# Three moves in a fused attention and gated-MLP kernel: a reordered start, product sums spaced differently, and a DRAM reload placed behind weight slabs

## The chip, the cores and the metric

The kernel runs on one core of a Trainium2 chip. The metric is the device time of one execution in microseconds, the median of several runs. Runs of one kernel mostly agree within about 0.1%. Block 0 to block 3 are quarters of 512 tokens of the 2048-token sequence; "slab" is a 1 MB piece of weights in a ring of five buffers.

## The reference, cut to what matters

```python
x = A_x                                              # 1 x 2048 x 1024, bf16
x = x + _A_ref(_layernorm(x), A_wqkv, A_wo)          # attention over 8 keys, 2 apart, 32 heads of 32
x = x + _B_ref(_layernorm(x), W_gate, W_up, W_down)  # relu(x W_gate) * (x W_up), then W_down; 3584 wide
x = x + _A_ref(_layernorm(x), A_wqkv, A_wo)
x = x + _B_ref(_layernorm(x), W_gate, W_up, W_down)
```

## The kernel before: the parts that matter

The kernel is a list of events with planned times. They are sorted and emitted, and each engine's instructions stand in its queue in that order. VectorE's work is chained by `dv`, SyncE's transfers by `sp_dma`. While TensorE does block 0's gate and up projections, VectorE does block 1's attention in between. The scores of block 1 (`s`, product sums of q and k) go through DRAM to be regrouped by head: `store_s`, then `load_s`.

```python
def load_s(n):                         # the reload: 4 transfers, 256 KB each, packets of 256 bytes
    def f():
        sd = s_d[n % 2]
        s4 = work.tile([P, DG, W, P], BF16, tag="t", name=f"s4_{n}")
        for tq in range(TPB):
            src = bass.AP(tensor=sd.tensor, offset=sd.offset + tq * P,
                          ap=[[DG * W * BLK, H], [BLK, DG * W], [1, P]])
            sp_dma(s4[32 * tq:32 * tq + 32, :, :, :].rearrange("p d w t -> p (d w) t"), src)
        att[n]["s4"] = s4
    return f

def head_sum(n):                       # u: what waits for the reload, on VectorE
    s4 = att[n].pop("s4")
    u = work.tile([P, DG // 2, W, P], F32, tag="ac", name=f"u_{n}", bufs=1)
    dv(nc.vector.tensor_tensor, u[:], s4[:, 0:2], s4[:, 2:4], op=ALU.add)
    ...

def gu_steps(n, ln):                   # gate group j and up group j, 8 matmuls of 512 columns each
    ...
            for nm in ("g", "u"):
                acc = psum.tile([P, BLK], F32, tag="acc", name=f"acc_{nm}")   # 6 buffers in all
                ...                                                           # relu on ScalarE
    def gate(j):
        def f():                       # hT(j): frees the up buffer; on VectorE, behind all that is emitted before
            dv(nc.vector.tensor_tensor, hold["hT"][:, j, :], ups.pop(j)[:], rs.pop(j)[:], op=ALU.mult)
        return f
    ...
```

The start, `ln_first`, normalises the first four tiles of 128 tokens, turns them on TensorE and copies them out, while `v_first` already multiplies by the V weights. Its code is in the diff below.

## Time and profile before

| | before |
|---|---|
| median, lowest, highest of all 6 runs | 1617.99, 1617.71, 1619.53 us |
| profiled span | 1616.4 us |
| TensorE busy | 1611.3 us |
| first V matmul; first matmul of the Q projection | 8.09; 24.04 us |
| reload issued; u starts | 233.90; 243.90 us |
| slab w_u(4) issued, lands; its first weight load; its first matmul by the chain | 239.88, 246.9; 247.06; 247.43 us |

The lines of the profile are in the prediction. How to read the table: TensorE never waits after the start, so other engines cost nothing as long as their results are in time. What counts in such a kernel is the slack of each hand-over: by how much a transfer or a VectorE result is early.

### The profile page before, as it was taken

The page shows a single profiled execution, that of the slowest core. Times are in us where ns is not written, and L with a number is a line of the kernel's source. Part 1 is how long each engine was busy: PE and PEld are TensorE (multiplying, and loading weights), DVE is VectorE, ACT ScalarE, POOL GpSimd, SP SyncE. Part 2 cuts the span into 40 slices and gives each one's busy share as a digit, 9 for nine tenths or more (in the row PEclk, how much of TensorE's full clock was granted, in tenths as well). Part 3 has the DMA queues.
Part 4 walks back from the last instruction along what each step waited for, and adds up shares of the span by engine and source line. Part 5 has one row for each costly group of instructions (what it writes and reads, how often), then busy time and mean ns, then how long its engine had stood idle before and what let it go on. Part 6 is the DMA issues. An engine that isn't in the chain of part 4 may idle for free.

```text
span 1616.4 us, 18930 instructions
## 1 busy us (share of the span) xinstructions
PE 1611.3 (100%) x7633; PEld 786.6 (49%) x7633; DVE 1137.1 (70%) x960; ACT 475.8 (29%) x968; POOL 180.4 (11%) x168
## 2 busy tenths in 40 slices
PE   9999999999999999999999999999999999999999
PEld 6646544444444445444454444544445444444444
DVE  5999989996989698929489293893939939311211
ACT  5853312132116313603136031361313311131110
POOL 2400100010003002300053000530005100000000
PEclk9999999999999999999999999999999999999999
DMA  9868868697669766794847947479574794755452
GB/s 306 180 190 238 224 159 262 183 216 204 208 192 217 200 184 212 192 246 146 227 160 201 240 153 230 152 205 252 165 226 155 203 245 157 209 161 177 157 167 68
DMA packets 407448, 317.92 MB, mean 197 GB/s; under 512 B 166464, under 2 KB 387008, under 8 KB 406848
## 3 DMA queue, kind: packets, MB, share of 16 engines
q1 hardware_dynamic: 406784, 316.13, 69.9%
q8 instruction: 59, 0.97, 0.3%
q10 hardware_dynamic: 576, 0.59, 0.1%
q14 instruction: 29, 0.24, 0.0%
HBM read 266.29 MB, written 34.66 MB: 186 GB/s over the span
## 4 chain that ended last, share of the span: by engine, by line
PE 99%; DMA 0%; ACT 0%; DVE 0%; issue 0%; ACTq 0%; DVEq 0%
PE acc_u L132 24%; PE acc_g L132 24%; PE dacc L132 18%; PE acc_v L132 7%; PE acc_wo L132 7%; PE acc_k L132 7%; PE acc_q L132 7%; PE dacc_pair L132 6%; DMA x<-in_A_x_dram 0%; ACT xn_first L328 0%; PE tp_pair L385 0%; PE L L132 0%; DVE x L837 0%; DVE xnT_first L106 0%; ACTq L175 0%
## 5 line engine op out<-in xcount | busy, mean ns | idle before, releaser
L132 PE MATMUL acc_g<-xnT_b,w_g 128*128 128x512 bf16 x1792 | 423.3, 379 | 0.0
L132 PE MATMUL acc_u<-xnT_b,w_u 128*128 128x512 bf16 x1792 | 423.3, 379 | 0.0
L790 ACT ACTIVATE r<-acc_g 128x512 bf16<-128x512 f32 x224 | 133.5, 596 | 726.7 <-PE acc_g L132 701.6
L106 DVE TENSOR_TENSOR hT<-acc_u,r 128x512 bf16<-128x512 f32 x224 | 150.5, 685 | 240.7 <-PE acc_u L132 238.2
L132 PE MATMUL dacc<-w_d,hT 128*128 128x512 bf16 (+1 forms) x1400 | 301.9, 375 | 0.0
L132 PEld LDWEIGHTS <-hT 128*128 128x128 bf16 x1820 | 178.1, 98 | 208.9
L132 PEld LDWEIGHTS <-w_u 128*128 128x128 bf16 x1792 | 175.3, 98 | 211.5
L132 PEld LDWEIGHTS <-w_g 128*128 128x128 bf16 x1792 | 175.4, 98 | 211.4
L106 DVE TENSOR_TENSOR pv<-a,vhm 128x4096 bf16<-128x4096 bf16 x64 | 143.4, 2281 | 0.0
L837 DVE TENSOR_TENSOR x<-dacc,x 128x512 bf16<-128x512 f32 (+1 forms) x38 | 24.5, 672 | 154.2 <-PE dacc L132 154.2
L608 DVE TENSOR_TENSOR t<-q,k 128x2048 f32<-128x2048 bf16 x56 | 128.0, 2292 | 6.7 <-ACT k L543 4.6
L106 DVE TENSOR_TENSOR t<-q,k 128x2048 f32<-128x2048 bf16 x56 | 127.4, 2285 | 3.7 <-ACT k L543 2.6
L106 DVE TENSOR_TENSOR pv<-pv 128x1024 bf16<-128x1024 bf16 (+1 forms) x128 | 113.6, 947 | 0.0
L549 POOL COPY kh<-k 128x14 bf16<-128x14 bf16 x40 | 56.0, 1406 | 504.3 <-ACT k L543 504.3
L132 PE MATMUL acc_wo<-w_o,oT 128*128 128x512 bf16 x512 | 111.8, 379 | 0.0
L621 DVE TENSOR_TENSOR ac<-ac,t 128x2048 f32<-128x2048 f32 x48 | 109.6, 2284 | 0.3
L106 DVE TENSOR_TENSOR ac<-ac,t 128x2048 f32<-128x2048 f32 x48 | 109.5, 2282 | 0.0
L264 POOL TENSOR_TENSOR st_b<-st_b,neg_half 128x1 f32<-128x1 f32 x29 | 43.9, 1523 | 525.8 <-ACT st_b L263 525.7
L132 PE MATMUL dacc_pair<-w_d,hT 128*128 128x512 bf16 x420 | 95.9, 379 | 0.0
L132 PEld LDWEIGHTS <-oT 128*128 128x128 bf16 x512 | 50.0, 98 | 60.4
L259 ACT ACTIVATE xn_b<-x 128x1024 bf16<-128x1024 bf16 x29 | 30.3, 1045 | 129.1 <-DVE x L106 67.0
L446 ACT CAST vT<-acc_v 128x512 bf16<-128x512 f32 x56 | 32.8, 588 | 57.6 <-PE acc_v L132 56.6
(134 smaller groups left out, 1230.0 us busy)
## 6 DMA issues: line engine op xcount, KB each, us to landing
w_g<-in_B_W_gate_dram SPq DMA_DIRECT2D x56, 1024.0 KB, 7.4
w_u<-in_B_W_up_dram SPq DMA_DIRECT2D x56, 1024.0 KB, 5.5
w_d<-in_B_W_down_dram SPq DMA_DIRECT2D x48, 1024.0 KB, 5.7
w_o<-in_A_wo_dram SPq DMA_DIRECT2D x16, 1024.0 KB, 7.0
vhm<-v_d SPq DMA_DIRECT2D x32, 284.0 KB, 6.8
v_d<-vT SPq DMA_DIRECT2D x8, 1024.0 KB, 9.8
oT<-o_d SPq DMA_DIRECT2D x32, 256.0 KB, 4.5
w_d<-in_B_W_down_dram SPq DMA_DIRECT2D x16, 512.0 KB, 3.9
```

What stands on the lines that cost most here:

```text
L106: tail_dve[0] = f(*args, **kwargs).ins
L132: tail_pe[0] = nc.tensor.matmul(*args, **kwargs).ins
L259: nc.scalar.activation(xn, xt[:], ACT.Square, accum_out=sq)
L264: nc.gpsimd.tensor_tensor(rstd, vpe, neg_half[:, 0:1], op=ALU.pow)
L446: tail_act[0] = nc.scalar.copy(st["vT"][:, c, :], acc[:]).ins
L549: nc.gpsimd.tensor_copy(khalo[n][:, c, :], k[:, BLK:BLK + HALO])
L608: nc.vector.tensor_tensor(t[:], i0, i1, op=ALU.mult)
L621: nc.vector.tensor_tensor(o, ac[:], t[:], op=ALU.add)
L790: tail_act[0] = nc.scalar.activation(rs[j][:], acc[:], ACT.Relu).ins
L837: run = dv if n < NB - 2 else (lambda f, *args, **kwargs: f(*args, **kwargs))
```

## The change

The intent: let TensorE start a little earlier (ScalarE copies tile 0 out before it does statistics), and make the up slab w_u(4), which comes at most half a microsecond before it is needed, safe by putting it ahead of the reload. The product sums of block 1 are spaced differently too. The core of the diff:

```diff
-            elif t == 2:
-                nc.scalar.dma_start(x_tiles[t][:], x_dram[t * P:(t + 1) * P, :])
...
-    load_x(0, range(TPB - 1))
+    load_x(0, [0, 1])
...
-                sp_dma(tv[:, rows, :], src[:, rows, :])
+                start = nc.scalar.dma_start if (key[1], i) == (0, 1) else sp_dma
+                start(tv[:, rows, :], src[:, rows, :])
...
     load_slab(("v0", 0), qkv_half(2, 0))
-    load_x(0, [TPB - 1])
+    load_x(0, [2, 3])
...
-        act_square(2)
-        act_mean(2)
         bn(1, 0)
         ...
         copy(0, "a", 0, KC // 4, KC // 2)
+        act_square(2)
+        act_mean(2)
...
-        def second(h):
-            turn(1, (h,))
-            if h == 0:
-                copy(1, "v", 0)
-                return
+        def second():
+            turn(1)
+            copy(1, "v", 0)
             copy(1, "v", 1)
+            bn(3, 0)
+            act_power(2)
+            bn(3, 1)
+            aggr(3)
             apply(2)
-            act_square(3)
-            act_mean(3)
-            act_power(3)
             apply(3)
...
-                if kc == KC // 2 - 1:
-                    ln["second"](0)
                 for c in range(KC):
                     prod(kc, c, 0, 1)
-            ln["second"](1)
+            ln["second"]()
...
-    spread(sums1[6:10], t_fill + 1.4, 4.6)
+    spread(sums1[6:10], t_fill + 3.3, 4.0)
...
-            ev.append((at + 40.5, load_s(1)))
+            ev.append((at + 24 * GRP + 0.5, load_s(1)))
```

I call its three parts the start, the sums (the `spread` line) and the reload (the last line). In the reload part SyncE's order becomes store, two small gets, w_u(4), w_g(5), reload; before it was store, get, reload, get, w_u(4), w_g(5).

More of the change, by code (lines that the diff above doesn't have):

```diff
@@ L373, in ln_first, with turn @@
         tps = {}
-        def turn(t, halves=(0, 1)):
-            if t in tps:
-                pass
-            elif t == 0:
+        def turn(t):
+            if t == 0:
                 tps[t] = [psum.tile([P, KC // 2, P], BF16, tag="acc", name=f"tp{h}")[:] for h in range(2)]
@@ L382, in turn @@
                 tps[t] = [both[:, h, 0:KC // 2, :] for h in range(2)]
-            for c in (h * (KC // 2) + i for h in halves for i in range(KC // 2)):
+            for c in range(KC):
                 with pe_group():
@@ L408, in ln_first @@
         copy(0, "v", 1)
-        act_power(2)
         apply(1, 0)
         apply(1, 1)
-        def second(h):
-            turn(1, (h,))
-            if h == 0:
-                copy(1, "v", 0)
-                return
+        def second():
+            turn(1)
+            copy(1, "v", 0)
             copy(1, "v", 1)
+            bn(3, 0)
+            act_power(2)
+            bn(3, 1)
+            aggr(3)
             apply(2)
-            act_square(3)
-            act_mean(3)
-            act_power(3)
             apply(3)
```

## The prediction

> **What bounds the kernel now.** I read the page first. Its part 1 says that TensorE is busy 1611.3 of 1616.4 us, and its part 4, the chain that ended last, is 99% PE.
>
> ```profile
> PE 1611.3 (100%) x7633; PEld 786.6 (49%) x7633; DVE 1137.1 (70%) x960; ACT 475.8 (29%) x968; POOL 180.4 (11%) x168
> PE 99%; DMA 0%; ACT 0%; DVE 0%; issue 0%; ACTq 0%; DVEq 0%
> ```
>
> A busy PE may still hide gaps, so I took the chain of waits in order of time. From 24.04 us on it is matmuls in steps of 1.73 us for 8 of 512 columns (216 ns each); the 56 groups of block 0's gate and up take 287.15 - 190.45 = 96.70 us, or 56 x 1.727: no gap. The waits of PE in the whole trace are two, both at the start (1.5 and 0.4 us). So time can be won only before 24 us, at most some tenths, and lost anywhere that a buffer or slab becomes late. The start, from the chain (start us, us, what):
>
> ```profile
> 1.25 4.17 DMA x<-in_A_x_dram
> ...
> 5.45 1.16 ACT xn_first L328 x2
> ...
> 6.63 1.15 ACT xn_first L328 x2
> 7.78 0.27 ACT xnT_first L328
> ...
> 8.09 1.50 PE acc_v L132 x24
> 9.59 0.33 PE tp_pair L385 x4
> ...
> 9.94 0.43 DVE xnT_first L106
> ...
> 10.42 0.38 PE tp_pair L385 x4
> 10.80 3.53 PE acc_v L132 x48
> ```
>
> See two things: ScalarE does tile 2's two statistics passes (5.45 to 7.78) before it may copy tile 0's turned half, and TensorE waits for that copy; and the second four transposes of tile 1 stand behind a VectorE copy (9.94).
>
> The other half of the change is at 230 to 252 us, inside block 0's gate/up. From the timeline:
>
> ```profile
> 181.09 2.55 POOL L301 TENSOR_TENSOR rstd<-vpe,neg_half 128x1 f32<-128x1 f32 x1 [3.48 <-DVE vpe L106]
> ...
> 185.35 0.54 DVE L106 TENSOR_SCALAR xn_b<-x,mv,rstd 128x1024 bf16<-128x1024 bf16 x1
> ...
> 230.59 2.48 DVE L106 TENSOR_TENSOR hT<-acc_u,r 128x512 bf16<-128x512 f32 x4
> ...
> 233.90 4.38 SPq L121 DMA_DIRECT2D s<-s_d  x4
> 239.88 0.39 SPq L121 DMA_DIRECT2D w_u<-in_B_W_up_dram  x1
> 243.90 2.29 DVE L106 TENSOR_TENSOR u<-s 128x2048 f32<-128x2048 bf16 x1 [0.85 <-DMA s<-s_d]
> ...
> 266.07 1.28 DVE L106 TENSOR_TENSOR hT<-acc_u,r 128x512 bf16<-128x512 f32 x2
> ```
>
> The four reloads of the sums hold SyncE's in-order queue, and the up slab behind them is issued only at 239.88; it lands 7.0 us later (246.9), and TensorE starts on it at 247.43. Half a microsecond to spare: late, but not yet a wait.
>
> **What the Trainium skill says.** (1) "DMA: Bandwidth & Descriptors", Issuing engines are not separate DMA queues: copies started by ScalarE and SyncE run on the same 16 engines and interleave; a second issuer saves only issue time. The trace agrees: from 3 to 5 us the two queues divide the engines (58% to 63% SyncE's, 36% to 46% ScalarE's), and the total is 0.35 to 0.41 MB per us either way. (2) "SBUF - State Buffer", Who interferes with whom: a VectorE instruction with two SBUF inputs and a GpSimd instruction that reads SBUF block each other. The trace agrees: the power above took 2.55 us beside a 2.29 us VectorE product, and 0.55 us where VectorE stood idle. (3) "DMA: Bandwidth & Descriptors", Why small descriptors are slow: packets of 256 bytes pay a fixed overhead. The trace agrees: the sums' reload ran at some 165 GB/s, slabs at 350 to 400.
>
> **The change part by part.**
>
> *First copy.* ScalarE's two passes over tile 2 (1.06 + 0.19 us each) go behind the copies. Tile 0's first four transposes end at 7.37; with 0.06 us of semaphore the copy starts at 7.43 instead of 7.68, and the first V matmul at 7.84 instead of 8.09: **-0.25 us**. The first V quarter must be there: 1.57 MB (x tiles 0 and 1, two quarters) instead of 1.33 MB come in before it is sure, 0.24 MB at 0.38 MB/us is 0.6 us later than its landing at 6.7 (issue 1.72 + 5.0): estimate 7.4, just in time. The second quarter, on ScalarE's queue, comes before it is needed.
>
> *Tile 1 turned at once.* 32 matmuls at 56 ns (24 took 1.34 us to issue) from 7.84 end at 9.62. The two halves of tile 1's normalisation end at 9.45 and 9.78, as before: they hang on GpSimd's power (8.45), not on ScalarE. So the last four transposes start at 9.84 and end at 10.23; the build shows that the first copy now waits for all eight (as for tile 2, where the copy started at 14.85, after the eighth ended at 14.78). It runs 10.29 to 10.71, and the next 48 matmuls start at 10.76. Before, by the timeline, they started at 10.64. **+0.12 us**: the 0.25 is given back, since before the eight matmuls of the fourth row filled the copy's time.
>
> *Tiles 2 and 3.* x2 is now behind the first quarter and lands at about 8.3 (1.83 MB at 0.38 MB/us and the same delay). Square and mean end at 10.7; VectorE runs the copies to 11.1, tile 3's statistics (2 x 0.69 + 0.21) and tile 2's variance; apply(2) at 13.0 to 13.6 against its transposes at 14.3; apply(3) at 14.7 against 17.4. Both hidden. VectorE's added 1.6 us - 0.2 us and ScalarE's saved 2.5 us cost nothing.
>
> *Block 1's product sums.* The instruction order shows one move on VectorE: the last xn_b comes before a product and a sum instead of after. It gains the transposes of xnT_b four us, which nobody needed. But VectorE now stands idle for the power: 0.82 us from vpe to xn_b (as measured at 176.82 and 177.64) instead of running on, less 0.07: everything after it, back to back until 230.59, is **0.75 us later**. Gate buffers are six; their order of reuse in the build gives gate group j the buffer that hT(j-4) frees. hT(8) ended at 231.28, group 12 starts at 231.89: slack 0.6 us. With 0.75: **+0.2 us** of PE wait.
>
> *Reload behind the slab.* w_u(4) and w_g(5) go first, at about 232.8: the slab's slack grows from 0.5 to 8 us, worth nothing here as PE did not wait. The reload loses: 2.1 MB at 350 GB/s are 6.0 us from 234.1 to 240.1, then the 1 MB in small packets (7 us as before, when it moved from 235.2 to 242.2), landing 1.6 us later: u at 248 to 248.6 instead of 243.9. VectorE is nearly back to back from there to 311, so hT(19), which ended at 266.75, ends at some 271.2; gate group 23 needs it at 269.88. Slack 3.1 against a shift of 4 to 4.7: **+0.9 to 1.6 us**, less the 0.2 already lost. oT for block 1 (landed at 307.1, needed at 311) just holds.
>
> *Sum:* 0.12 + 0.2 + 0.7 to 1.4, or about +1.0 to 1.7 us of 1618 by the full working.
>
> **The rivals.** (a) The reload interleaves better with the slabs, or is issued before the second slab is through, so that its shift is under 3 us: nothing is lost at group 23 and the change is +0.1 to +0.3 us. For it: the 1.6 us of landing and the 7 us of moving are estimates, and 3.1 us of slack is near. (b) The start gains: in runs where x2 lands later than in this profile, ScalarE's passes delay the copy more (one of three runs took 1619.53), and the new order is free of that; then up to -0.4 us, 1617.7. Against it: tile 1's normalisation, on GpSimd and VectorE, sets 10.7 whatever ScalarE does. (c) The first V quarter, now sharing with ScalarE's 0.5 MB, lands after 7.8 and the start loses up to 0.5 us. For it the estimate of 7.4 is near; against it PE has no need before 7.84. (d) The start holds and the slab, issued earlier, spares waits of slower runs: a gain of tenths in the median.
>
> **Range and chances.** My sum says 1619.1 to 1619.8, rivals (a), (b) and (d) 1617.6 to 1618.3. I choose 1618.8, between them and nearer to the sum; 8 in 10 from 1617.0 to 1620.6. 2% is 32 us, and no term comes near: even all terms with the wrong sign stay under 5 us. Within 2%: 0.985; faster 0.005; slower 0.01.
>
> **What would show it.** In the changed profile: the first V matmul near 7.8 instead of 8.09, and the 48 near 10.76 instead of 10.64; a VectorE wait of some 0.7 us for rstd before the last xn_b, the power taking 0.55 instead of 2.55 us; w_u(4) issued near 233; VectorE's wait for s near 5 us, u at 248; and PE waits at gate group 12 (0.2 us) and 23 (about 1 us). If u starts before 247 or group 23 shows no wait, that step is wrong. If the 48 start before 10.5, the copy did not wait for all eight transposes. A change of over 5 us would mean that a slab or the output tail moved, of which I see no sign.

## The result, and the profile after

| | before | after |
|---|---|---|
| median, lowest, highest of 6 runs | 1617.99, 1617.71, 1619.53 | 1622.67, 1621.62, 1623.62 us |
| profiled span | 1616.4 | 1621.7 us |
| first matmul of the Q projection | 24.04 | 23.70 us |
| reload issued; u starts | 233.90; 243.90 | 234.65; 252.66 us |

The change makes the kernel slower: the ratio is 1.0028, with a 95% interval of 1.0016 to 1.0041. (A ratio is the mean time of one kernel's fast runs over that of the other's in the same rounds, so not quite the ratio of the medians.) This is within 2%, but it is a clear 4.7 us, and outside the range that I gave.

The waits of TensorE, from the view of who waited for whom, after (us in total, times, longest):

```profile
PE acc_u L132 <- DVE hT L106: 2.9, 2, 1.8
PE scratch L132 <- DVE ones L309: 1.5, 1, 1.5
PE acc_g L132 <- DVE hT L106: 1.1, 1, 1.1
PE acc_wo L132 <- DVE x L106: 1.0, 1, 1.0
...
```

The two lines left out (0.6 and 0.5 us) belong to the start, like the second line. The other three are new, and all three are waits for VectorE: for the gate products hT and, in the output projection, for the residual sums x. They are four waits, 2.9 + 1.1 + 1.0 = 5.0 us. The view counts each of them from the modelled end of the matmul before, which overlaps the next one's start by 0.16 us (groups of 8 are shown 1.89 us long and follow each other in steps of 1.73), so the four cost some 0.6 us more than it says. The start was 0.34 us earlier (23.70 instead of 24.04), and 5.0 + 0.6 - 0.3 = 5.3 us is the whole difference of the two profiled spans (1621.7 - 1616.4). The medians differ by a little less, 4.68 us: the profiled run of the changed kernel is one of its two longest. The timeline shows where the waits fall, and what VectorE did meanwhile:

```profile
234.65 12.33 SPq L121 DMA_DIRECT2D s<-s_d  x4
...
252.66 2.29 DVE L106 TENSOR_TENSOR u<-s 128x2048 f32<-128x2048 bf16 x1 [9.96 <-DMA k<-k_d]
...
256.13 0.68 DVE L106 TENSOR_TENSOR hT<-acc_u,r 128x512 bf16<-128x512 f32 x1
256.87 1.89 PE L132 MATMUL acc_g<-xnT_b,w_g 128*128 128x512 bf16 x8 [1.15 <-DVE hT L106]
259.81 0.68 DVE L106 TENSOR_TENSOR hT<-acc_u,r 128x512 bf16<-128x512 f32 x1
260.55 1.89 PE L132 MATMUL acc_u<-xnT_b,w_u 128*128 128x512 bf16 x8 [1.79 <-DVE hT L106]
...
275.58 1.89 PE L132 MATMUL acc_u<-xnT_b,w_u 128*128 128x512 bf16 x8 [1.06 <-DVE hT L106]
```

The number in square brackets is the idle time just before the instruction, with what ended it. VectorE stood idle for 9.96 us in front of u. (The trace names a get of k as what ended it; u's semaphores are those of the four reloads, and the last of these was issued at 245.78 and landed 6.8 us later, at 252.6.) The gate products stand behind u in VectorE's in-order queue, so they come late, and TensorE runs out of accumulators (e9 below tests this).

### The profile page after: what moved, and what is told of

Read it like the earlier page. It is cut to its first block, busy times and chain, and to the rows that moved or that the text cites. A ratio compares the mean times of both kernels' runs of the same rounds, so it can differ in the third digit from the quotient of the medians.

```text
span 1621.7 us, 18928 instructions
## 1 busy us (share of the span) xinstructions
PE 1610.8 (99%) x7633; PEld 786.4 (48%) x7633; DVE 1138.2 (70%) x962; ACT 473.4 (29%) x964; POOL 179.0 (11%) x168
## 4 chain that ended last, share of the span: by engine, by line
PE 89%; DVE 7%; DMA 1%; issue 1%; SPq 1%; POOL 0%; ACT 0%; DVEq 0%; POOLq 0%
PE acc_g L132 21%; PE acc_u L132 21%; PE dacc L132 17%; PE acc_v L132 7%; PE acc_q L132 7%; PE acc_wo L132 6%; PE dacc_pair L132 6%; PE acc_k L132 5%; DVE pv L106 2%; DVE ac L106 2%; DVE t L106 1%; SPq L121 1%; DVE hT L106 1%; DMA w_g<-in_B_W_gate_dram 1%; DVE x L106 0%
```

## The experiments

Each run is shown with its edit against the kernel before or the changed one. The times in brackets after "before" are of the same job on the same chip.

### One part at a time

`e1_start` is the kernel before with the start of the change only, `e2_reload` with the reload only, `e3_sums` with the sums only, and `e4_no_reload` is the changed kernel with this edit:

```diff
-            ev.append((at + 24 * GRP + 0.5, load_s(1)))
+            ev.append((at + 40.5, load_s(1)))
```

> Only the start of the change (second V quarter on ScalarE's queue, tile 2 later, tile 1 turned at once). My theory: the whole loss of 4.7 us comes from the reload behind the slabs, so this run shows no PE wait after 25 us, and the reordering itself costs +0.1 us from the first bn_stats to the 48 matmuls (6.74 us instead of 6.64): 1617.6 to 1618.2 us. If the 0.44 us earlier landing of x tile 0 seen in the changed kernel belongs to the change, bn_stats starts near 3.56 here too and the time is 0.3 us below before; if it is chance, it starts anywhere from 3.5 to 4.0. Rival, that the start shifts VectorE against TensorE and so makes later waits: over 1619.

> Only the reload of block 1's sums moved behind the two slabs. My theory: the four reloads are issued over some 12 us instead of 4.4, u starts near 252 instead of 243.9, and TensorE waits in gate groups 19 to 24 and in the output projection for 4.5 to 5 us: 1622 to 1623 us. Rival, that the 0.75 us later VectorE of the new sums' spacing is needed as well: a loss of 4 us or less.

> Only the new spacing of block 1's product sums. My prediction had +0.2 us from a wait at gate group 12; the changed kernel's trace shows no such wait, so now I expect none: 1617.7 to 1618.3 us, with VectorE's wait of 0.66 us for rstd and hT(8) 0.75 us later. By the prediction: 1618.2 and a PE wait near 232.

> The change with the reload put back ahead of the slabs. My theory: no PE wait after 25 us, 1617.5 to 1618.2 us, so the reload carries all of the loss. Rival, that the start or the sums carry part: over 1619 us.

Measured (before: 1618.27 us, 9 runs):

| run | median us | ratio, 95% interval | u starts | new PE waits after 25 us |
|---|---|---|---|---|
| e1_start | 1618.30 | 1.0003, 0.9990 to 1.0015 | 244.63 | none in the view of PE; see below |
| e2_reload | 1621.78 | 1.0021, 1.0008 to 1.0035 | 251.72 | 3.8 us, for VectorE |
| e3_sums | 1619.46 | 1.0006, 0.9994 to 1.0019 | 245.34 | 0.9 us, for the slab w_u(4) |
| e4_no_reload | 1618.62 | 1.0002, 0.9990 to 1.0015 | 244.71 | 0.3 us, for the slab w_u(4) |

The reload alone brings 3.5 of the 4.7 us, and without it nothing clear of noise is left. So the reload is the cause of the loss. It may not bring all of it: with the sums, VectorE is later still (u at 252.66 instead of 251.72) and the waits are 5.0 instead of 3.8 us. (The medians alone do not tell 3.5 from 4.7 us: the intervals of the two ratios overlap.) My rival for e2, that the sums are needed for part of it, was right by that much.

The sums held a surprise that neither I nor the expectation had. The waits of `e3_sums`:

```profile
PE scratch L132 <- DVE ones L310: 1.5, 1, 1.5
PE acc_u L132 <- DMA w_u<-in_B_W_up_dram: 0.9, 1, 0.9
...
```

With the new spacing the sums are stored later, the reload is issued at 234.86 instead of 233.90, and the slab behind it, issued at 241.21 instead of 239.88, comes too late. This shows what the reload move was for. The interval of the medians does not resolve it; the wait in the trace does. The slab was even nearer to its limit than the 0.5 us of the chain say. In e1, whose edit is at the start only, it was issued at 240.52, and the weight load, which the view of PE's waits does not count, waited for it; the matmuls behind slipped by 0.2 us. Weight loads of w_u(4) before and in e1:

```profile
247.06 1.61 PEld L132 LDWEIGHTS <-w_u 128*128 128x128 bf16 x8
247.61 1.41 PEld L132 LDWEIGHTS <-w_u 128*128 128x128 bf16 x8 [0.55 <-DMA w_u<-in_B_W_up_dram]
```

The start: from the first `bn_stats` to the first of the 48 matmuls it took 6.64 us before, 6.74 us after and 6.73 us in e1 (4.03 to 10.76). The reordering costs 0.1 us, as predicted. The rest of the 0.34 us is chance: the first `bn_stats`, which waits for x, started at 4.00 before and 3.56 after, but also at 4.03 in e1 (new start) and at 3.54 and 3.50 in e2 and e3 (old start).

### Half the bytes, and lateness without the bytes

`e5_between` puts the reload behind w_u(4) but ahead of w_g(5):

```diff
-            ev.append((at + 40.5, load_s(1)))
...
             events.append((ends[i - RING] + 0.3 ..., lambda key=key, src=src: load_slab(key, src)))
+            if key == ("u", 0, 4):
+                events.append((events[-1][0], load_s(1)))
```

`e6_late9` and `e7_late4` leave the transfers alone and keep VectorE busy in front of u, with 8 or 4 additions:

```diff
         s4 = att[n].pop("s4")
+        if n == 1:
+            idle = soft.tile([P, W, P], F32, tag="d", name="idle")
+            dv(nc.vector.memset, idle[:], 0.0)
+            for _ in range(8):
+                dv(nc.vector.tensor_tensor, idle[:], idle[:], idle[:], op=ALU.add)
```

`e8_actq` is the reload alone moved, but started from ScalarE's queue (`nc.scalar.dma_start` in `load_s(1)`).

> The kernel before with the reload behind one slab, w_u(4), and ahead of the other, w_g(5). In the run with the reload alone moved, u started 7.8 us later (251.7) and TensorE lost about 3.8 us, so some 4 us of lateness are free. One slab ahead of the reload is half of the bytes: u near 247 to 248 us, no PE wait on VectorE, no wait for w_u(4): 1617.6 to 1618.2 us, and no run above 1618.8 if the slab's half microsecond of slack is what spreads the runs of before. Rival, that the order of queueing and not the bytes makes the reload late: u near 251 and 1621 us.

> The kernel before, transfers untouched, with a memset and eight 128x1024 float32 additions on a spare tile put on VectorE just before u (some 10 us, of which 0.85 us was idle anyway): u near 253. My theory, that the loss is VectorE's lateness and nothing else of the transfers: PE waits for hT in gate groups 19 to 24 and for x in the output projection, 4.5 to 5.5 us in sum, 1622.5 to 1623.5 us. Rival, that the reload's contention with slabs and gets costs part: under 3 us.

> The same with four additions (some 5.2 us, u near 248.3, 4.4 us later), which is the lateness that the prediction reckoned with. By the prediction's slack of 3.1 us at gate group 23: a PE wait of 0.9 to 1.3 us there, 1619.0 to 1619.4 us. By the slack that the changed kernel shows (9.1 us late, 5.0 us lost): 0.3 us or nothing, 1617.9 to 1618.5 us.

> The reload at its new place, but started from ScalarE's queue, so that its descriptors do not stand behind the slabs' on SyncE's. Theory A, that the lateness is the queue: the four issues took 12.3 us because SyncE's queue was full of slab descriptors, and the engines ran dry near 245 to 246: then here each issue takes under 2 us, u starts by 248 and TensorE loses under 1 us (ScalarE's relu may wait a little behind the issues). Theory B, that the engines' bandwidth alone makes it late: u near 251 as before, 1621 to 1622 us.

Measured (before: 1618.48 us, 9 runs):

| run | median us | ratio, 95% interval | u starts | PE waits after 25 us |
|---|---|---|---|---|
| e5_between | 1618.67 | 1.0004, 0.9992 to 1.0017 | 247.91 | 0.5 us, x in the output projection |
| e7_late4 | 1621.25 | 1.0018, 1.0003 to 1.0034 | 249.32 | 2.3 us, for hT |
| e6_late9 | 1625.56 | 1.0045, 1.0032 to 1.0059 | 253.65 | 5.2 us, for hT |
| e8_actq | 1631.92 | 1.0084, 1.0070 to 1.0097 | 259.86 | 10.0 us, for hT and relu |

Half the bytes ahead of the reload make u 4.0 us later, all of them 7.8 us (e2). So each megabyte of slab makes the reload about 4 us later, and the first 4 us are almost free. From the timeline of `e5_between`:

```profile
234.18 8.02 SPq L121 DMA_DIRECT2D s<-s_d  x4
...
247.91 2.29 DVE L106 TENSOR_TENSOR u<-s 128x2048 f32<-128x2048 bf16 x1 [4.92 <-DMA s<-s_d]
```

e6 and e7 show that a late u costs TensorE time with no transfer moved; the rival that the transfers' contention itself costs part is not needed. Both lost more than I expected, though, and for different reasons. In e7 the accumulators come free in another order: its up group 20 waited for the third hT behind u (261.74 to 262.42; the group started at 262.48), while in the changed kernel up group 20 started at 264.00, before the third hT (265.10). So its free lateness is 5.2 - 2.3 = 2.9 us (5.4 us by the clock, less 0.2 because its TensorE was that much later), where the changed kernel has 9.1 - 5.0 = 4.1 us (8.8 us by the clock, and 0.3 more because its TensorE was that much earlier). The slack is thus a property of one build, not of the design alone. In e6 the waits are as expected, 5.2 us, but the time is 7.1 us longer. The table of stretches of e6 shows why (columns: stretch, its length, then busy time of PE, PEld, DVE, ACT and POOL with counts, the granted TensorE clock, the DMA share and GB/s):

```profile
255.00:257.80 2.80, 0.82 (x4) 0.29 (x3) 2.77 (x4) 0.00 (x0) 0.00 (x0) 1.00 1.08 344
257.80:261.40 3.60, 3.45 (x8) 1.15 (x8) 3.56 (x3) 0.51 (x1) 0.00 (x0) 0.53 0.06 19
```

After a wait of 2.02 us the granted clock was 0.53, and the next eight matmuls took 3.45 us instead of 1.89: 1.6 us more for one wait. In the changed kernel's waits of 1.15 and 1.79 us it stayed at 1.00.

e8 gave no support to the idea that the reload was late because it stood behind slab descriptors in one queue. With ScalarE's own queue three of the issues took 10.9 us, u started at 259.86, and ScalarE's relus stood still for that time:

```profile
235.20 10.92 ACTq L638 DMA_DIRECT2D s<-s_d  x3
246.22 1.58 ACT L790 ACTIVATE r<-acc_g 128x512 bf16<-128x512 f32 x3 [11.09 <-DMA s<-s_d]
```

So the forecast of Theory A failed by 12 us, and Theory B's 251 does not fit either. But e8 is no clean test of either: SyncE, freed from the reload, went on to issue gets and the next two slabs (w_u(5) at 244.0), which shared the engines with it.

### Is a full queue slower than its bytes?

`e11_wait_slab` makes SyncE wait, ahead of the reload, until the second slab has landed, by a small copy out of it:

```diff
+    mark = dram.tile([P, 8], BF16, name="mark")
...
             sd = s_d[n % 2]
+            if n == 1:
+                sp_dma(mark[:], slab[("g", 0, 5)][:, 0, 0:8])
```

> The changed kernel with a 2 KB copy out of the slab w_g(5) put ahead of the reload, so that SyncE issues the reload only when both slabs have landed and its queue is empty. In the changed kernel the reload's issue took 12.3 us, w_g(5) landed only at 246.6 and the last piece at 252.6. If the full queue made the reload slower than its bytes: the slab lands by 241.5, the four issues take 4.4 us, the reload 9.9 us as in the kernel before, u near 251 or earlier and the time is below 1622. If the bytes alone decide: u at 252.5 or later, 1622.5 us or more.

Measured: 1626.27 us (before: 1618.05; ratio 1.0050, 1.0034 to 1.0067), u at 255.30.

```profile
233.49 0.45 SPq L121 DMA_DIRECT2D w_u<-in_B_W_up_dram  x1
234.04 0.53 SPq L121 DMA_DIRECT2D w_g<-in_B_W_gate_dram  x1
244.66 0.34 SPq L121 DMA_DIRECT2D mark<-w_g  x1
245.09 4.90 SPq L121 DMA_DIRECT2D s<-s_d  x4
```

The reload then took 10.2 us from issue to u (245.09 to 255.3), against 10.0 us before (233.90 to 243.90), and the issue took 4.9 us, nearly as short as before (4.4). But the second slab landed only at 244.6 (234.04 + 10.6), where I had reckoned 240.1; most of its bytes had moved by 242.5, and only 0.04 MB came after. So u was 2.6 us later than in the changed kernel; 0.5 us of that comes from the sums, which this run stored later (231.75 instead of 231.22). Waiting for an empty queue costs more than it saves.

It does not follow that the reload moved as fast behind the slabs. Its packets are the only ones of 256 bytes in this stretch, so the packet records of the traces show when it moved. From the first packet to the last it took 7.2 us before (235.25 to 242.44) and 7.9 us in e11 (246.41 to 254.31), but 10.0 us in the changed kernel (241.24 to 251.19) and in e2 (240.17 to 250.22). The DMA view of the changed kernel, from 241 to 245, from 245 to 246.5 and from 246.5 to 251.5 us:

```profile
DMA packets 1985, 0.70 MB, mean 175 GB/s; under 512 B 1723, under 2 KB 1985, under 8 KB 1985
DMA packets 303, 0.07 MB, mean 50 GB/s; under 512 B 303, under 2 KB 303, under 8 KB 303
DMA packets 2700, 1.05 MB, mean 211 GB/s; under 512 B 2207, under 2 KB 2700, under 8 KB 2700
```

In the middle stretch the engines moved next to nothing, with half of the reload's 4096 packets still to come; SyncE's third issue of the reload, begun at 241.15, ended only at 245.74. So 2 to 3 us of the lateness are a slower reload. Whether the full queue or something else behind the slabs slows it is not shown: e11 takes away both the slabs and the queue. The wait of 3.26 us that TensorE had here was again followed by half clock (0.50 from 259 to 264 us), which is why the time is longer than the lateness alone would make it.

### Gate products ahead of u, and the slab ahead of the store

`e9_later_u` is the changed kernel with the attention of block 1 planned later in VectorE's order:

```diff
-            spread(softmax_steps(1), at + 52.0, 3.6)
-            spread(pv_steps(1), at + 63.0, 5.3)
+            spread(softmax_steps(1), at + 61.0, 3.6)
+            spread(pv_steps(1), at + 71.0, 4.4)
```

`e10_slab_first` is the changed kernel with the reload back at `at + 40.5`, and w_u(4) loaded at `t_gu0 + 37.4`, just ahead of the store of the sums:

```diff
+            when = t_gu0 + 37.4 if key == ("u", 0, 4) else ends[i - RING] + 0.3 if i >= RING else 0.1 * i
```

> The changed kernel with the softmax and value products of block 1 planned 8 to 9 us later in VectorE's order, so that gate products 15 and 16 stand before u and not behind it. Theory, that TensorE loses because gate products wait in VectorE's in-order queue behind the late reload: the PE waits of 1.15 and 1.79 us at 257 and 260 us vanish; VectorE has still lost some 9 us, so the later waits (1.06 near 275 us, 1.04 in the output projection) stay or grow: 1619.0 to 1621.5 us. Rival, that the waits come of the total of VectorE's work before the output projection: no gain, 1622 to 1623 us.

> Start and sums as in the change, but the reload stays ahead of w_g(5), and w_u(4) is issued ahead of the store of the sums. The slab is then safe (issued near 231, needed at 247), and the reload has one slab ahead: u near 247.5 to 248.5 us. With one slab ahead in the earlier run u was 4.0 us late and 0.5 us were lost: so 1618.0 to 1619.0 us and no wait for w_u; a wait for x in the output projection of up to 0.8 us. Rival, that a safe slab is worth nothing: the same time as the run with start and sums alone (1618.6).

Measured (before: 1618.30 us, 9 runs): e9 1623.43 us (1.0030, 1.0016 to 1.0043), e10 1618.26 us (0.9999, 0.9986 to 1.0013). The waits of e9, of which the last two belong to the start:

```profile
PE acc_wo L132 <- DVE x L106: 3.5, 1, 3.5
PE scratch L132 <- DVE ones L309: 1.5, 1, 1.5
PE acc_v L132 <- DMA w_v<-in_A_wqkv_dram: 0.7, 1, 0.7
PE acc_v L132 <- DVE xnT_first L106: 0.5, 1, 0.5
```

The gate waits are gone, so they were indeed a matter of standing behind u. But the lost VectorE time was paid later, in one wait of 3.5 us in the output projection, and the half clock after it (0.53 from 317 to 323 us) made the following 47 matmuls 13.17 us long instead of 10.30. Its four runs spread from 1621.04 us (mean clock 1.000) to 1624.90 us (0.998), so not every execution seems to pay for the clock. My expectation of 1619.0 to 1621.5 missed; the rival, that VectorE's total before the output projection counts, was nearer. The wait of 0.7 us for V weights is the case that the prediction named as its rival (c): in this run x came early (bn_stats at 3.55) and the first V weights did not.

In e10 w_u(4) is issued at 230.07, u starts at 246.06, and TensorE waits for nothing after the start. Its five runs lie between 1618.12 and 1618.43. So the slab can be made safe without a loss by putting it ahead of the store, where SyncE had nothing to do, and not between the store and the reload. u is 1.4 us later than in e4 (244.71), which is the same kernel without the move of the slab. It is no faster than the kernel before; the runs point to no version that is.

## Why the prediction was wrong

Its point, 1618.8 us, and its range to 1620.6 lay below the measured 1622.67. The mechanism was named: a reload behind two slabs makes VectorE late, and gate products behind it starve TensorE. Step by step:

- **First copy and tile 1 turned at once** (-0.25, then +0.12): right. The reordering costs 0.1 us (6.73 us in e1 against 6.64). The first V matmul came at 7.39 instead of 7.84 only because x landed 0.44 us earlier, by chance. The copy did wait for all eight transposes: they ended at 9.78, and it started at 9.82.
- **Tiles 2 and 3 hidden**: right. Their transposes came in the flow of matmuls, with no wait.
- **Sums**: the 0.75 us and the cause were nearly right: before the last xn_b VectorE waited 0.66 us, the power took 0.55 us, and hT(8) started at 231.11, or 0.86 us later relative to TensorE. The wait at gate group 12 was wrong: there was none. (I had taken one order of accumulators for all groups, which may be why; no run tests it.) The true cost was elsewhere: the slab's slack, which I had written down as 0.5 us and which was 0.2 us to the weight load, is smaller than 0.75 us. e3 shows that wait, 0.9 us. In the full change the reload's move hides it.
- **Reload behind the slab, the term that failed**: "2.1 MB at 350 GB/s are 6.0 us from 234.1 to 240.1, then the 1 MB in small packets ... landing 1.6 us later: u at 248 to 248.6". Measured: u at 252.66. Of the three terms, the first was small in error: the reload's first packet moved at 241.2, 1.1 us later than 240.1 (the DMA engines started slowly, at 182 GB/s from 234 to 237, and then reached 371). The second failed: I took over the 7 us of the kernel before, and the reload moved for 10.0 us, with the engines nearly dry from 245 to 246.5. The landing took 1.4 us (251.2 to 252.6), about as forecast. 1.1 + 3.0 - 0.2 = 3.9 us, and with 0.1 us from the landing to u this is the distance from 248.6 to 252.66. So the shift was 8.8 us and not 4 to 4.7.
- **What the shift costs**: I put it at gate group 23, with 3.1 us of slack. The waits came at gate and up group 19, at up group 23 and in the output projection, with 4.1 us free in sum by the view (3.4 us if the 0.6 us that the view leaves out is counted). So with the true shift the prediction would have said 9.1 - 3.1 = 6 us, near the loss. That the slack fits is partly luck, since three of the four waits were at other places.
- **Rival (a)**, a better interleaving, is partly true: the reload's first packet moved at 241.2, before the second slab landed (246.6). It did not save the case, since the reload was then slower. **Rival (c)** happened in one run (e9, 0.7 us). **Rivals (b)** and **(d)** brought nothing that shows in a median.

What stays open: why the reload moved more slowly behind the slabs, and why the DMA engines ran nearly dry from 245 to 246.5 us while it was still being issued.

## What to carry to other kernels

Before a transfer is moved behind others, do not add bytes over the best bandwidth to a moving time measured with free engines (here that gave 4 to 4.7 us, and 8.8 were measured); try it in a run of its own, as e2 and e5 did. Then compare the lateness with the smallest slack of what waits for it, over the whole stretch in which the waiting engine has no idle time. Look for a third place in the queue: here the slab fitted ahead of the store, where it delayed u by 2.2 us against the kernel before, while some 3 to 4 us of lateness were free (e7, e5). And where one engine is busy 99.7% of the time, a change can win little and lose wherever it eats more than a slack, so list the slacks before listing the savings.

## What the Trainium skill lacked or had wrong

- "TensorE: Matmul & The Clock Gate", The HAM clock gate, gives as the condition for the slow clock one idle window of about 3.4 us. Here a single wait of 2.02 us between dense matmuls was followed by a granted clock of 0.53 for 3.6 us (e6), and waits of 3.26 and 3.49 us by 0.50 and 0.53 (e11, e9); waits of 1.15 and 1.79 us were not (the changed kernel). A wait of 2 us can cost 1.6 us on top.
- "DMA: Bandwidth & Descriptors", Issuing engines are not separate DMA queues, says that another issuer saves only issue time. The runs agree that nothing else is gained (e8), but the page lacks the price: behind busy engines three issues held ScalarE for 10.9 us, and its relus with it.
- "DMA: Bandwidth & Descriptors" has no figure for a transfer queued behind others. Here each 1 MB slab ahead made a 1 MB reload in packets of 256 bytes 4 us later (e5, e2), where 1 MB at the 350 GB/s that slabs reach is 3.0 us; the reload itself moved for 10.0 us behind two slabs, and for 7.2 us with none ahead.
